# Twelve of sixteen maximum scans of w_in moved from the second attention stage into units 32 to 39 of the first

## The chip, the cores and the metric

One core of a Trainium2 chip runs the whole program. The metric is device time in microseconds (us), the median of three runs. TensorE (PE) does the matrix products and transposes, VectorE (DVE) and ScalarE (ACT) the elementwise work, GpSimd (POOL) a few additions and small casts, and the queue of SyncE (SP) issues every transfer. Each engine works through its own instructions in a fixed order and waits on semaphores of the others.

## The reference, cut to what matters

Attention with a learned position bias, then an MLP with a squared ReLU. The setup is four batches, eight heads, 576 positions, head width 64, and an MLP from 512 to 2048 and back.

```python
scores = scale * np.matmul(q, k.transpose(0, 1, 3, 2))
h = np.maximum(x @ w1 + b1, 0.0)          # x: log distance over log position
scores = scores + (h @ w2).transpose(2, 0, 1)[None]
attn = np.exp(scores - np.max(scores, axis=-1, keepdims=True))
attn = attn / (np.sum(attn, axis=-1, keepdims=True) + 1e-09)
x = np.matmul(attn, v)                    # rows of all heads side by side
r = np.maximum(x @ w_in, 0.0)
return (r * r) @ w_out
```

## The kernel before, in words

Attention is cut into 80 **units**: a batch b, a pair of heads hp and a chunk ic of 128 query rows (chunk 4 is the short tail of 64 rows). Units 0 to 39 take batches 0 and 1, chunk by chunk: the tail chunk in units 0 to 7, then chunks 0, 1, 2 and 3 in units 8 to 15, 16 to 23, 24 to 31 and 32 to 39. Units 40 to 79 take batches 2 and 3, five units for each pair of heads and batch. The MLP follows.

A unit has these steps. `score_products` (L421) writes two pairs of PSUM banks, `sp`, of which there is one set: the products of the next unit wait until VectorE has read those of this one. `softmax` reads them with one VectorE instruction for each head (L431, two in a full unit, one in a tail unit), and ScalarE takes the exponential (L436). Two units later TensorE transposes the result (L524, L516), ScalarE copies it (L827 in the first stage, L1041 in the second), and TensorE multiplies by v (L542); VectorE copies the sum to `xT` (L555). At the end of a head pair the row sums are inverted (L448, L449) and multiplied in (L491).

In units 0 to 30 the bias network runs beside this: VectorE masks (L371) and products (L387), TensorE sums (L381), GpSimd additions into the bias table (L395). Its tiles lie in the pool `prep`. It has nothing left to do from unit 31 on.

The MLP works on scaled halves of w_in and x. The scale of w_in comes from its largest absolute value: `scan_w` (L202, one VectorE reduction over 512 columns) for each of 16 tiles of 512 KB, that are fetched only for this (L662), then `top_w`. Before the change all 16 scans run in the second stage, as a job from unit 41 on, with five tiles in flight; `scan(k)` fetches the tile five further on into the place that it has just read. Only once all are done do the other jobs follow: `get` fetches the weights again, `in_job` splits them (L193 on ScalarE, L195, L196, L198, L199 on VectorE, L706 to L708 and L720 on GpSimd, L718 on ScalarE, L724 on VectorE), and `x_scaled` splits x (L765 on GpSimd, L771 on ScalarE, L778 on VectorE).

Two things set the order. In units 0 to 39 a scheduler places the instructions on each engine, by its own estimate of when each could start; only the score products are pinned. From unit 40 on the order is written by hand: `fill` takes jobs in the order of their list into each unit, as long as the allowance `room["DVE"]` (1.65 us more for each full unit, 2.5 for a tail unit) is not used up. `dest_at` says from which unit the first halves of w_in may be written over parts of the bias table that are no longer read.

Of the kernel before, what the change touches and what calls it, by code (L numbers as in the profile page):

```python
# [27 lines left out]
AB = 2  # L28
# [49 lines left out]
def attention_then_relu2_mlp(ctx: ExitStack, tc: tile.TileContext, q, k, v, cols, w_in, w_out, psi, xmat, dist, out):  # L78
# [729 lines left out]
    def ends(u):  # L808
        b, hp, ic = units[u]
        return ic == (chunks[-1] if u < NA else NIC - 1)  # L810

    rest = theta_steps(128, 512)[2:]
    for s in range(NA):
        loads(s)
        scores(s)
# [21 lines left out]

    prep_stack.close()
    half_stack.close()
# [79 lines left out]
    def scan(k):  # L919
        scan_w(k)  # L920
        if k + len(raws) < NF:
            fetch_in(ins[k + len(raws)], raws[k % len(raws)])
        if k == NF - 1:
            jobs.insert(len(norms), [now[0] + 1, [("DVE", 0.75, lambda: power_job(now[0] + 1, top_w(), scaled))]])
            for n in early[:4]:
                get(n)
            for _ in range(3):
                next_job()
            job(now[0], ("SP", 0, lambda: get(2), lambda: all((0, m) in xs_t for m in ORDER)))
# [15 lines left out]
    def x_scaled(n, ps_col):  # L945
        scale_of(n, ps_col)
        if n == 0:
            place_x = raw_tile("w2")
            free = [place_x[:, 512 * k:512 * k + 512] for k in range(2)]
            for k, ms in enumerate(((3, 1, 7), (4, 6), (2, 5))):  # L950
                stages = []
                for m in ms:
                    if RIGHT[m][1]:
                        sum_at[m] = free[k].rearrange("p (c t) -> p c t", c=2)
                        stages.append(("POOL", 1.3, lambda m=m: sums_x(0, (m,))))
                    stages.append(("ACT", 0.71, lambda m=m: high_x(0, (m,))))
                    stages.append(("DVE", 0.74, lambda m=m: low_x(0, (m,))))
                jobs.insert(len(norms), [now[0], stages])

    dest_at = [53] + [60] * 6 + [70]  # L960
    order = list(early[:7]) + [2, early[7], 3]
# [49 lines left out]
    with tc.manual_schedule():  # L1011
        job(NA + 1, *(("DVE", 0.68, lambda k=k: scan(k)) for k in range(NF)))
        x_job(NA + 4, 0)
# [6 lines left out]
        for s in range(NA, NU + TL + 2):  # L1020
            now[0] = s
            full = s < NU and units[s][2] < TAIL
            room["DVE"] = min(room.get("DVE", 0), 0.3) + (1.65 if full else 2.5)
            room["ACT"] = min(room.get("ACT", 0) + (0.55 if full else 1.9), 0.6 if full else 1.5)
            loads(s)
            if s == NA:
                for m, tag in enumerate(raws):
                    fetch_in(ins[m], tag)
            if s < NU:
# [292 lines left out]
```

## Time and profile before

| | |
|---|---|
| median of three runs | 724.46 us (724.44 to 724.8) |
| profiled execution | 724.39 us |
| its span, first to last instruction | 722.6 us |
| PE busy | 691.2 us, 96% |
| VectorE busy | 554.6 us, 77% |
| ScalarE busy | 474.8 us, 66% |
| GpSimd busy | 186.6 us, 26% |
| granted TensorE clock | full speed in every stretch to 700 us |

Unit 32 begins at about 161.8 us, unit 40 at 189.5 us, and the MLP at 343.4 us. The 1.8 us between the span and the profiled execution's time lie around the program. A table of stretches shows busy time of each engine in a stretch; where TensorE's busy time is short of the stretch, or its units are further apart than in other stretches with the same work, time is lost.

### The profile page before, as it was taken

The page shows a single profiled execution, that of the slowest core. Times are in us where ns is not written, and L with a number is a line of the kernel's source. Part 1 is how long each engine was busy: PE and PEld are TensorE (multiplying, and loading weights), DVE is VectorE, ACT ScalarE, POOL GpSimd, SP SyncE. Part 2 cuts the span into 40 slices and gives each one's busy share as a digit, 9 for nine tenths or more (in the row PEclk, how much of TensorE's full clock was granted, in tenths as well). Part 3 has the DMA queues.
Part 4 walks back from the last instruction along what each step waited for, and adds up shares of the span by engine and source line. Part 5 has one row for each costly group of instructions (what it writes and reads, how often), then busy time and mean ns, then how long its engine had stood idle before and what let it go on. Part 6 is the DMA issues. An engine that isn't in the chain of part 4 may idle for free.

```text
span 722.6 us, 17384 instructions
## 1 busy us (share of the span) xinstructions
PE 691.2 (96%) x6966; PEld 565.0 (78%) x6966; DVE 554.6 (77%) x1165; ACT 474.8 (66%) x954; POOL 186.6 (26%) x313
## 2 busy tenths in 40 slices
PE   7799999999999999899999999999999999999992
PEld 6577777787777877678878888888888888888881
DVE  8998888775588999889898969777468875566761
ACT  5678778777587888798666766666465564454220
POOL 6563433331110156444332304112011111000000
PEclk9999999999999999999999999999999999999997
DMA  6640000004449521410613333050067303533100
GB/s 187 200 123 3 19 2 2 3 2 118 169 162 286 163 85 36 136 60 14 236 59 161 147 160 117 8 212 1 1 201 294 134 14 134 187 117 117 59 2 29
DMA packets 31620, 75.13 MB, mean 104 GB/s; under 512 B 5556, under 2 KB 13876, under 8 KB 30516
## 3 DMA queue, kind: packets, MB, share of 16 engines
q1 hardware_dynamic: 31540, 74.03, 30.5%
q8 instruction: 55, 0.90, 0.5%
q14 instruction: 25, 0.20, 0.1%
HBM read 55.66 MB, written 18.35 MB: 102 GB/s over the span
## 4 chain that ended last, share of the span: by engine, by line
PE 79%; DVE 12%; ACT 4%; issue 2%; DMA 1%; ACTq 0%; DVEq 0%
PE y L1198 26%; PE ha L1103 12%; PE sp L421 9%; PE px L542 9%; PE hb L1103 9%; PE pp L524 8%; PE bb L381 4%; DVE t L431 2%; DVE mask L371 2%; ACT pt L1041 1%; PE pa L516 1%; ACT p L436 1%; DVE bt L387 1%; DMA raw<-in_w_in 1%; DVE wa L198 1%
## 5 line engine op out<-in xcount | busy, mean ns | idle before, releaser
L1103 PEld LDWEIGHTS <-area 128*128 128x128 f16 x1680 | 147.7, 98 | 25.1 <-issue 8.4
L1198 PE MATMUL y<-w,gh 128*128 128x512 f32 x576 | 149.1, 398 | 1.2 <-ACT gh L1142 1.2
L431 DVE CUSTOM_DVE_ANT_0 t<-sp,area 128x576 f32<-128x576 f32 x144 | 104.3, 752 | 26.0 <-PE sp L421 16.6
L1198 PEld LDWEIGHTS y<-w,gh 128*128 128x128 f32 x576 | 105.0, 188 | 23.4 <-ACT gh L1142 2.2
L436 ACT ACTIVATE p<-t,negm 128x576 f32<-128x576 f32 x144 | 111.9, 787 | 12.5 <-DVE negm L431 11.8
L421 PE MATMUL sp<-k,q 64*128 64x288 f32 (+1 forms) x640 | 98.5, 425 | 4.0 <-DVE negm L431 3.2
L542 PE MATMUL px<-pt,v 128*64 128x128 f32 (+1 forms) x1600 | 92.2, 266 | 1.6 <-DVE xT L491 0.8
L542 PEld LDWEIGHTS px<-pt,v 128*64 128x64 f32 x1600 | 79.2, 137 | 17.6 <-ACT pt L1041 7.1
L1103 PE MATMUL ha<-area 128*128 128x256 f16 (+1 forms) x816 | 84.8, 260 | 0.3 <-DVE c L1120 0.3
L524 PE MATMUL pp<-ident,p 128*128 128x128 f32 x576 | 78.9, 277 | 2.9 <-DVE xT L491 1.7
L1198 PE MATMUL y<-w,gl 128*128 128x512 f32 x288 | 79.0, 390 | 0.0
L395 POOL TENSOR_TENSOR area<-bt,bt 128x256 f32<-128x256 f32 x72 | 53.6, 767 | 78.5 <-DVE bt L387 78.5
L524 PEld LDWEIGHTS pp<-ident,p 128*128 128x128 f32 x576 | 62.2, 141 | 13.2 <-issue 7.5
L421 PEld LDWEIGHTS sp<-k,q 64*128 64x128 f32 (+1 forms) x640 | 53.3, 175 | 24.3 <-issue 5.7
L1103 PE MATMUL hb<-area 128*128 128x256 f16 (+1 forms) x612 | 65.0, 260 | 0.0
L1198 PEld LDWEIGHTS y<-w,gl 128*128 128x128 f32 x288 | 54.1, 188 | 12.2 <-DVE gl L1143 0.2
L371 DVE TENSOR_TENSOR mask<-sdist,theta 128x1024 f16<-128x1024 f16 x81 | 55.8, 726 | 5.6 <-PE bb L381 5.2
L381 PEld LDWEIGHTS <-mask 128*128 128x128 f16 x1296 | 42.3, 100 | 12.2 <-DVE mask L371 6.8
L381 PE MATMUL bb<-wmov,mask 128*128 128x64 f16 x1296 | 47.4, 196 | 4.4 <-DVE mask L371 4.1
L1041 ACT COPY pt<-pp 128x512 f32<-128x512 f32 x76 | 41.1, 602 | 15.2 <-PE pp L524 15.1
L827 ACT COPY pt<-pp 128x512 f32<-128x512 f32 x68 | 37.7, 588 | 14.4 <-PE pp L524 14.4
L1143 DVE TENSOR_TENSOR gl<-area,gh 128x512 fp32r<-128x512 f32 (+1 forms) x40 | 25.4, 668 | 26.3 <-ACT gh L1142 24.2
(164 smaller groups left out, 987.7 us busy)
## 6 DMA issues: line engine op xcount, KB each, us to landing
raw<-in_w_in SPq DMA_DIRECT2D x32, 512.0 KB, 4.5
r<-in_w_out SPq DMA_DIRECT2D x16, 512.0 KB, 5.5
xs<-area SPq DMA_DIRECT2D x4, 1792.0 KB, 11.9
py<-o SPq DMA_DIRECT2D x12, 512.0 KB, 2.7
o<-py SPq DMA_DIRECT2D x12, 512.0 KB, 4.4
v<-in_v SPq DMA_DIRECT2D x16, 320.0 KB, 4.2
q<-in_q SPq DMA_DIRECT2D x32, 128.0 KB, 3.0
out<-o SPq DMA_DIRECT2D x8, 512.0 KB, 2.9
```

The costliest lines, as they stand in the source:

```text
L371: DVE.tensor_tensor(out=out, in0=win, in1=th, op=ALU.is_ge)
L381: PE.matmul(bb[:, 64 * (7 - r):64 * (8 - r)], lhsT=m[:, r], rhs=wmov[:, n], start=(n == 0), stop=(n == 1))
L395: POOL.tensor_tensor(out=dst, in0=tw, in1=sw, op=ALU.add)
L421: mm = PE.matmul(out_t[to, x, :HALF], lhsT=qt[rows, cols], rhs=kt[rows, k0:k0 + HALF], start=True, stop=True)
L431: DVE.tensor_tensor_reduce(out=t.rearrange("p (x n) -> p x n", x=2), in0=sp[:, :, :HALF], in1=bias.rearrange("p (x n) -> p x n", x=2), sca ...
L436: ACT.activation(out=p[:, S * n:S * n + S], in_=t, func=AF.Exp, bias=negm[:, n:n + 1], scale=-1.0, accum_out=sums[:, 2 * ic + n:2 * ic + n ...
L524: PE.transpose(pp[:, 128 * c:128 * c + 128], p[:, k0:k0 + 128], ident)
L542: PE.matmul(px[64 * h:64 * h + 64, 128 * m:128 * m + w], lhsT=vt[:, c, h], rhs=src, start=(c == 0), stop=(c == 4))
L827: ACT.copy(dst, src)
L1041: ACT.copy(*c)
L1103: PE.matmul(h[:, s, :w], lhsT=a, rhs=x, start=(k == 0), stop=(k == 5))
L1198: PE.matmul(y_t[n][k], lhsT=(gl if m == 2 else gh)[:, slot, o:o + 128], rhs=wl if m == 1 else wh, start=((n, P) in firsts and f == 0 and m ...
```

## The change

Twelve of the sixteen scans are taken out of the job of the second stage. `scan_first` is called at the start of each of units 32 to 39: at unit 32 it closes `prep`, opens the pool `scan` of five tiles in its place and fetches five tiles; at units 34 to 39 it makes two scans each and fetches into the tiles that are scanned. The four last tiles are fetched at unit 40 and scanned as before. The allowance of VectorE per full unit becomes 1.5 us. The first destinations of w_in are free from unit 50, where it was 53, and the splits of x start at unit 51 at the earliest.

```diff
--- before.py
+++ after.py
@@ -809,8 +809,23 @@
         b, hp, ic = units[u]
         return ic == (chunks[-1] if u < NA else NIC - 1)
 
+    scan_stack, SCANS = ExitStack(), 12
+
+    def scan_first(s):
+        n = s - AB * HP * TAIL
+        if n == 0:
+            prep_stack.close()
+            stage_p["scan"] = scan_stack.enter_context(tc.tile_pool(name="scan", bufs=1, side="left"))
+        fetched_now = range(5) if n == 0 else range(2 * n + 1, min(2 * n + 3, SCANS)) if n >= 2 else ()
+        for k in range(2 * n - 4, min(2 * n - 2, SCANS)) if n >= 2 else ():
+            scan_w(k)
+        for k in fetched_now:
+            fetch(ins[k], stage_p["scan"].tile([128, 1024], F32, name="raw", tag=f"s{k % 5}", bufs=1))
+
     rest = theta_steps(128, 512)[2:]
     for s in range(NA):
+        if s >= AB * HP * TAIL:
+            scan_first(s)
         loads(s)
         scores(s)
         if s and rest:
@@ -835,7 +850,7 @@
             if waiting and waiting[0][:2] != (b, hp):
                 scale_x(*waiting.pop(0))
 
-    prep_stack.close()
+    scan_stack.close()
     half_stack.close()
     aux_stack.close()
     bank_stack = ExitStack()
@@ -919,7 +934,7 @@
     def scan(k):
         scan_w(k)
         if k + len(raws) < NF:
-            fetch_in(ins[k + len(raws)], raws[k % len(raws)])
+            fetch_in(ins[k + len(raws)], raws[(k - SCANS) % len(raws)])
         if k == NF - 1:
             jobs.insert(len(norms), [now[0] + 1, [("DVE", 0.75, lambda: power_job(now[0] + 1, top_w(), scaled))]])
             for n in early[:4]:
@@ -955,9 +970,9 @@
                         stages.append(("POOL", 1.3, lambda m=m: sums_x(0, (m,))))
                     stages.append(("ACT", 0.71, lambda m=m: high_x(0, (m,))))
                     stages.append(("DVE", 0.74, lambda m=m: low_x(0, (m,))))
-                jobs.insert(len(norms), [now[0], stages])
-
-    dest_at = [53] + [60] * 6 + [70]
+                jobs.insert(len(norms), [max(now[0], first[groups[AB * HP + AB]] + 1), stages])
+
+    dest_at = [50] + [60] * 6 + [70]
     order = list(early[:7]) + [2, early[7], 3]
     raw_of = dict(zip(early, ("stage", "stage", "zw", "w3", "stage", "stage", "zw", "stage")))
     after = {early[0]: early[4], early[1]: early[5], early[2]: early[6], early[3]: 3, early[4]: early[7]}
@@ -1009,7 +1024,7 @@
 
     sum_at = {}
     with tc.manual_schedule():
-        job(NA + 1, *(("DVE", 0.68, lambda k=k: scan(k)) for k in range(NF)))
+        job(NA + 1, *(("DVE", 0.68, lambda k=k: scan(k)) for k in range(SCANS, NF)))
         x_job(NA + 4, 0)
         x_job(NA + 7, 1)
         for b, hp, rows_t in waiting:
@@ -1020,12 +1035,12 @@
         for s in range(NA, NU + TL + 2):
             now[0] = s
             full = s < NU and units[s][2] < TAIL
-            room["DVE"] = min(room.get("DVE", 0), 0.3) + (1.65 if full else 2.5)
+            room["DVE"] = min(room.get("DVE", 0), 0.3) + (1.5 if full else 2.5)
             room["ACT"] = min(room.get("ACT", 0) + (0.55 if full else 1.9), 0.6 if full else 1.5)
             loads(s)
             if s == NA:
-                for m, tag in enumerate(raws):
-                    fetch_in(ins[m], tag)
+                for m, tag in enumerate(raws[:NF - SCANS]):
+                    fetch_in(ins[SCANS + m], tag)
             if s < NU:
                 negm, sps = score_products(s, False)
             fill(s, 3)
```

The three places below show the built order. `raw` is a tile of w_in, `small` holds the columns of maxima, `sp` the score products, `t` the scores with bias, `xT` the attention output.

VectorE, from the copy behind the softmax of unit 31 to just ahead of the softmax of unit 33, before:

```order
L555 COPY xT_82<-px 128x128
L431 ISA t,negm<-sp,area 128x576
L431 ISA negm 128x1
L431 ISA t,negm<-sp,area 128x576
L431 ISA negm 128x1
L555 COPY xT_83<-px 128x128
L448 TENSOR_SCALAR sums<-sums 128x9
L449 RECIPROCAL sums<-sums 128x9
```

and after:

```order
L555 COPY xT_82<-px 128x128
L202 TENSOR_REDUCE small<-raw 128x1 x2
L431 ISA t,negm<-sp,area 128x576
L431 ISA negm 128x1
L431 ISA t,negm<-sp,area 128x576
L431 ISA negm 128x1
L202 TENSOR_REDUCE small<-raw 128x1
L555 COPY xT_83<-px 128x128
L202 TENSOR_REDUCE small<-raw 128x1
L448 TENSOR_SCALAR sums<-sums 128x9
L449 RECIPROCAL sums<-sums 128x9
L202 TENSOR_REDUCE small<-raw 128x1
```

The scheduler has put the first two scans ahead of the softmax of unit 32, and three more ahead of that of unit 33, though the code calls the first at unit 34; two stand ahead of each of the softmaxes of units 34, 35 and 36, and one ahead of that of unit 37.

The queue of SP, behind the last load of the bias network, before (k and q are the first loads for batch 2):

```order
L129 DMA xc<-in_xmat 128x576 x3
L154 DMA k_3507<-in_k 64x576
L155 DMA k_3507<-in_k 64x640
L167 DMA q_3510<-in_q 64x64
L168 DMA q_3510<-in_q 64x4x128
```

and after:

```order
L129 DMA xc<-in_xmat 128x576 x3
L662 DMA raw<-in_w_in 128x1024 x6
L154 DMA k_3527<-in_k 64x576
L662 DMA raw<-in_w_in 128x1024
L155 DMA k_3527<-in_k 64x640
L167 DMA q_3530<-in_q 64x64
L168 DMA q_3530<-in_q 64x4x128
L167 DMA q_3530<-in_q 64x64
L168 DMA q_3530<-in_q 64x4x128
L662 DMA raw<-in_w_in 128x1024 x2
```

The first fetch waits for the last addition of the bias network on GpSimd (L395). Seven fetches now stand ahead of or among the first group of k and q; the next two are followed by the second group, then three more by the third.

VectorE in units 66 and 67, from the inversion behind the softmax of unit 65 to just ahead of the softmax of unit 67, before:

```order
L448 TENSOR_SCALAR sums<-sums 128x9
L449 RECIPROCAL sums<-sums 128x9
L724 SCALAR_TENSOR_TENSOR area<-wa,small,area 128x256
L724 SCALAR_TENSOR_TENSOR area<-raw,small,area 128x640
L555 COPY xT_3903<-px 128x256
L431 ISA t,negm<-sp,area 128x576
L431 ISA negm 128x1
L431 ISA t,negm<-sp,area 128x576
L431 ISA negm 128x1
L778 SCALAR_TENSOR_TENSOR area<-raw,small,area 128x512
L724 SCALAR_TENSOR_TENSOR area<-wa,small,area 128x256
L724 SCALAR_TENSOR_TENSOR area<-raw,small,area 128x640
```

and after:

```order
L448 TENSOR_SCALAR sums<-sums 128x9
L449 RECIPROCAL sums<-sums 128x9
L724 SCALAR_TENSOR_TENSOR area<-wa,small,area 128x256
L724 SCALAR_TENSOR_TENSOR area<-raw,small,area 128x640
L555 COPY xT_3943<-px 128x256
L431 ISA t,negm<-sp,area 128x576
L431 ISA negm 128x1
L431 ISA t,negm<-sp,area 128x576
L431 ISA negm 128x1
L195 TENSOR_SCALAR wa<-wa 128x512
L196 TENSOR_SCALAR wa<-wa 128x512
```

Unit 66 holds the same work; in unit 67 two short conversions of weights stand where a split of x and two of w_in stood, since those splits have moved to earlier units.

## Rows read from the trace of the kernel before

**Rows 1.** The page: busy time and share of the span of each engine.

```profile
PE 691.2 (96%) x6966; PEld 565.0 (78%) x6966; DVE 554.6 (77%) x1165; ACT 474.8 (66%) x954; POOL 186.6 (26%) x313
```

**Rows 2.** Stretches: length; PE, PEld, DVE, ACT, POOL busy; clock, DMA share, GB/s.

```profile
161.80:189.50 27.70, 27.41 (x291) 20.64 (x290) 16.23 (x52) 20.65 (x54) 5.33 (x28) 1.00 0.42 117
203.30:254.90 51.60, 50.68 (x597) 40.65 (x591) 45.68 (x121) 39.88 (x103) 7.10 (x29) 1.00 0.71 215
272.00:309.70 37.70, 33.25 (x384) 26.37 (x384) 33.67 (x73) 31.29 (x76) 20.87 (x32) 1.00 0.26 82
```

**Rows 3.** TensorE in order of time, score products of units 32, 33, 34, 37.

```profile
161.79 1.24 PE L421 MATMUL sp<-k,q 64*128 64x288 f32 x8
...
165.34 1.24 PE L421 MATMUL sp<-k,q 64*128 64x288 f32 x8
...
168.88 1.24 PE L421 MATMUL sp<-k,q 64*128 64x288 f32 x8
...
179.43 1.24 PE L421 MATMUL sp<-k,q 64*128 64x288 f32 x8
```

**Rows 4.** VectorE in order of time: the softmax of unit 32, start of unit 33's.

```profile
163.22 0.76 DVE L431 CUSTOM_DVE_ANT_0 t<-sp,area 128x576 f32<-128x576 f32 x1 [2.15 <-PE sp L421]
...
163.90 0.75 DVE L431 CUSTOM_DVE_ANT_0 t<-sp,area 128x576 f32<-128x576 f32 x1
...
166.62 0.76 DVE L431 CUSTOM_DVE_ANT_0 t<-sp,area 128x576 f32<-128x576 f32 x1 [0.53 <-PE sp L421]
```

**Rows 5.** GpSimd in order of time: the last additions of the bias network.

```profile
157.51 2.10 POOL L395 TENSOR_TENSOR area<-bt,bt 128x256 f32<-128x256 f32 x3 [2.76 <-DVE bt L387]
```

**Rows 6.** The page, transfers: issues of w_in, KB each, median us to landing.

```profile
raw<-in_w_in SPq DMA_DIRECT2D x32, 512.0 KB, 4.5
```

**Rows 7.** The tile raw, 182 to 236 us: the scans' idle wait; landing times of fetches.

```profile
  DMA raw<-in_w_in: 1.1, 2
...
DMA to landing us min/median/max: 3.2/5.4/8.0
```

**Rows 8.** Stretches as in rows 2: k, q groups alone; fetches alone; both together.

```profile
163.00:178.00 15.00, 15.00 (x166) 11.71 (x166) 8.89 (x31) 10.98 (x28) 1.98 (x10) 1.00 0.47 124
190.00:194.00 4.00, 4.00 (x54) 3.10 (x52) 1.11 (x3) 2.46 (x7) 0.18 (x1) 1.00 1.00 395
218.00:226.00 8.00, 7.71 (x94) 5.89 (x90) 7.14 (x17) 5.39 (x16) 0.79 (x4) 1.00 1.08 238
```

**Rows 9.** Line L202, the scans of the second stage: min/median/max in ns.

```profile
L202 DVE TENSOR_REDUCE small<-raw x16: 629/680/686, 202.8 to 231.5; 128x1 f32<-128x512 f32 x16
```

**Rows 10.** TensorE in order of time, score products of units 42, 47, 57, 62, 67, 72, 77.

```profile
203.34 1.24 PE L421 MATMUL sp<-k,q 64*128 64x288 f32 x8
...
221.23 1.24 PE L421 MATMUL sp<-k,q 64*128 64x288 f32 x8
...
254.86 1.24 PE L421 MATMUL sp<-k,q 64*128 64x288 f32 x8
...
272.04 1.24 PE L421 MATMUL sp<-k,q 64*128 64x288 f32 x8 [0.20 <-DVE negm L431]
...
291.13 1.24 PE L421 MATMUL sp<-k,q 64*128 64x288 f32 x8 [0.94 <-DVE negm L431]
...
309.74 1.24 PE L421 MATMUL sp<-k,q 64*128 64x288 f32 x8 [0.20 <-DVE negm L431]
...
326.56 1.24 PE L421 MATMUL sp<-k,q 64*128 64x288 f32 x8
```

**Rows 11.** Line L199, the last step of a weight's conversion: min/median/max in ns.

```profile
L199 DVE SCALAR_TENSOR_TENSOR wa<-raw,wa x16: 691/692/1649, 252.0 to 575.4; 128x512 uint32<-128x512 uint32 x16
```

**Rows 12.** VectorE in order of time: splits of x and w_in ahead of unit 67's softmax.

```profile
290.90 1.52 DVE L778 SCALAR_TENSOR_TENSOR area<-raw,small,area 128x512 f16<-128x512 f32 x1
...
292.75 0.87 DVE L724 SCALAR_TENSOR_TENSOR area<-raw,small,area 128x640 f16<-128x640 f32 x1
```

**Rows 13.** GpSimd in order of time, in the same stretch.

```profile
290.61 1.27 POOL L765 TENSOR_TENSOR xT<-xT 128x512 f32<-128x512 f32 x1
```

## The prediction

> **What bounds the kernel now.** I read the page first: TensorE is busy for 96% of the span [rows 1], so time can only come from, or go into, stretches where it idles or its units stand further apart than they must. The table of stretches says where. While units 32 to 39 run, TensorE is busy for 27.41 of 27.7 us, VectorE for only 16.23 [rows 2]: there is room on VectorE, and none on TensorE. From 203.3 to 254.9 us, where the scans run now, TensorE is busy for 50.68 of 51.6 us; from 272.0 to 309.7 us for 33.25 of 37.7 [rows 2]. So the scans' own stretch loses little, and the loss sits later, among the splits of weights and x.
>
> The starts of the score products measure that loss with no model of busy time. Five units (four full, one tail) are one period, so starts five units apart hold the same work. Units 47 to 57 take 254.86 - 221.23 = 33.63 us, 16.8 for each five, and units 72 to 77 take 16.8 again [rows 10]: that is the clean period. Units 42 to 47 take 17.9, 57 to 62 take 17.2, 62 to 67 take 19.1 and 67 to 72 take 18.6 [rows 10]. Above 16.8 that is 1.1 + 0.4 + 2.3 + 1.8 = 5.6 us, all that a lighter VectorE can win back here. The rows at units 62, 67 and 72 name VectorE's softmax as what TensorE waited for.
>
> **What is removed.** Twelve scans of 0.68 us [rows 9] are 8.2 us of VectorE. They leave units 42 to 50, and from unit 47 on these already run at the clean period, though two scans waited 1.1 us in all for their fetches [rows 7]; what hides them there is TensorE's own work. Taking them out wins nothing at their place. What it does is let the later jobs start some four units sooner and, with 1.5 us instead of 1.65 a unit, lie thinner. 0.15 us less in 32 full units is 4.8 us of allowance, less than the 8.2 us of work gone, so nothing spills past the last unit.
>
> How much of the 5.6 us returns I read from the built order. In unit 67 two short conversions stand where three splits stood, as shown. In unit 63, too, a split of x and a pair of conversions (L195, L196) give way to nothing, and in unit 70 four conversion steps to two splits. But unit 66 holds the same work as before, unit 62 as well, and in unit 60 the pair L198 and L199 replaces the shorter L195 and L196. Three of the six heavy places get lighter, so I take half, **2.8 us gained**. The ends are 0 and 5.6: no loss, since VectorE has less to do in all, and no more than what is there.
>
> **What is added, and what waits.** The first fetch waits for the last bias addition, which ends at 157.51 + 2.10 = 159.6 us [rows 5]. The fastest fetch landed 3.2 us after its issue, the median one 5.4 [rows 7]. The first in an idle queue should be near the fast end; I take 3.4, which gives 163.1 us. Behind it, fetches alone move 395 GB/s [rows 8], so 512 KB [rows 6] follow each 1.33 us.
>
> VectorE meets the first scans too early. In the built order two stand ahead of the softmax of unit 32, which before began at 163.22 us and ended at 163.90 + 0.75 = 164.65 [rows 4]. Tile 1 lands at 163.1 + 1.33 = 164.4, its scan ends at 165.1, the two softmax instructions (1.43 us) at 166.5. Queued behind the waiting scan are that softmax and, on TensorE, the next score products, which need the PSUM that it reads: those of unit 33 go from 165.34 [rows 3] to 166.6, **1.2 us late**. Tiles 2 to 4 stand ahead of the softmax of unit 33. Tile 4 lands at 168.4, its scan ends at 169.1, the softmax at 170.5, and the products of unit 34 start at 170.6 in place of 168.88 [rows 3]: 1.7 late.
>
> The queue then sets the pace. Two more tiles are ahead of each of the next softmaxes, up to tile 10 ahead of that of unit 36, and by then two groups of k and q loads stand between them. These three groups moved in 163 to 178 us before, at a mean DMA share of 0.47 [rows 8]: 0.47 x 15 / 3 = 2.35 us of full transfer for a group. Tile 10 lands at 163.1 + 10 x 1.33 + 2 x 2.35 = 181.1, the softmax of unit 36 ends at 183.2, and the products of unit 37 begin at 183.3 instead of 179.43 [rows 3]: 3.9 late. TensorE has 0.3 us to spare in this stretch [rows 2], so the delay stays, and everything behind shifts with it.
>
> That sum lets k, q and fetches take turns without cost. The trace of before does not show them so in this stretch, but it has one with both, where the engines were full and moved 238 GB/s instead of 395 [rows 8]. If all from tile 5 (169.8 us) to tile 10 went at that rate, it would be five tiles of 0.524 MB and two groups of 124 GB/s x 15 us / 3 = 0.62 MB, 3.86 MB in 16.2 us. Tile 10 would land at 186.0 us, and the products of unit 37 come 8.8 us late. So the cost lies between 1.2 (only the first pair ever holds) and 8.8 us. I take **5.0 us lost**, nearer to 3.9 than to 8.8: tiles are fetched one by one as scans free them, so the mixture is not there all the time.
>
> Four other edits cost nothing on the path. k and q for unit 40 now stand behind seven tiles, 9.3 us at 1.33 each, and still land well ahead of 189.5 us, where that unit began. The four scans left have their places in units 42 to 45, which had scans before. The destination limit and the later of two starts for the splits only allow what the thinner jobs would use.
>
> **The sum.** 724.39 us of the profiled execution + 5.0 - 2.8 = 726.6. The median of the runs shown is 0.07 us above that execution, which changes nothing: **726.6 us**, 0.3% slower.
>
> **Rivals.** *The relief does not come.* The slow VectorE instructions may not be slow for want of allowance. L199 takes 0.69 us in the median and 1.65 once [rows 11]; ahead of unit 67 a split took 1.52 us while GpSimd added pieces of x [rows 12, 13], and a wider one behind it 0.87 [rows 12]. The additions move along with the splits, to units with as much softmax. Then only about 0.8 of the 2.3 + 1.8 us around units 62 to 72 is won, and 724.39 + 5.0 - 0.8 = 728.6, or 732 with the full mixture of loads. Against it: unit 63 and unit 67 have spare time now in which a slow split is harmless. The Trainium skill, page "SBUF — State Buffer", section "Who interferes with whom", has a rule for it: a VectorE instruction with two SBUF inputs contends with a GpSimd instruction that reads SBUF, and a reduction never does. By that rule the change takes away only work that never collided, and keeps all that did, which would give this rival's 728.6. The rows above agree as far as the splits go; the scans' narrow spread of 629 to 686 ns agrees too [rows 9].
>
> *Both effects cancel.* If the transfers keep to 395 GB/s and the softmaxes of units 35 and 36 find their tiles landed, the loss is about 3 us and the gain about 3: 724.4 us.
>
> *Faster: the scans hold only the first pair.* If k and q slip into gaps, every tile from the third on is there when VectorE arrives, and the loss is 1.2 to 2 us. If with it the thinner allowance clears most of the four slow periods, 4.5 us, the time is 724.39 + 1.5 - 4.5 = 721.4. It decides at tile 10: if that lands before about 178 us, the products of unit 37 are less than 1.5 us late. For it speaks that VectorE had 11 us idle in this stretch [rows 2]; against it, that twelve tiles alone need 16 us at the full rate after a start at 159.6.
>
> **How the numbers follow.** About 0.2% (1.45 us) is what a measurement of this kernel can tell from no change: faster is below 723.0, slower above 725.9. My forecast, a loss of 3.9 to 6.5 and a gain of 1.5 to 4, gets 0.45; it runs from 724.3 to 729.4, and 0.38 of it lies above 725.9. No relief gets 0.15, all slower. Cancelling gets 0.12, the same. The faster case gets 0.28. So slower 0.38 + 0.15 = 0.53, same 0.07 + 0.12 = 0.19, faster 0.28. The range for 8 in 10 leaves out the lower part of the faster case (0.12) and the upper part of no relief (0.06): 721.8 to 729.8 us. Both signs are in it; the forecast's own range is 724.3 to 729.4.
>
> **What would show it.** In the profile of the changed kernel VectorE should idle ahead of L202 for "DMA raw" between 161 and 186 us, some 5 us in all, and TensorE's score products of units 33 to 38 should wait for VectorE. Unit 37 should start near 184.5 us, 5 later than before. Periods of five units above 16.8 us between units 57 and 72 should add up to about 2.8 us. I am wrong if the first stage shows no idle VectorE ahead of the scans, or if those periods all come down to 16.8, or stay where they are.

## The result, and the profile after

The changed kernel takes 732.72 us (median of four, 732.09 to 734.15), the kernel before in the same comparison 724.45 us (724.44 to 724.8): ratio 1.0117, 95% interval 1.0101 to 1.0133. It is slower, as forecast, but by 8.3 us and not by 2.2, and outside the range of 721.8 to 729.8 us. The profiled execution took 733.0 us.

First the table of stretches, the lines that answer to [rows 2] (length; PE, PEld, DVE, ACT, POOL busy; clock, DMA share, GB/s): units 32 to 39, 42 to 56, 57 to 61 and 62 to 71.

```profile
162.06:198.30 36.24, 30.99 (x291) 23.59 (x290) 23.21 (x64) 20.56 (x54) 5.37 (x28) 0.91 0.87 258
212.10:264.82 52.72, 51.33 (x598) 41.10 (x594) 45.13 (x127) 42.88 (x108) 11.43 (x29) 1.00 0.31 95
264.82:283.97 19.15, 16.32 (x203) 12.87 (x204) 17.08 (x37) 15.58 (x41) 14.59 (x25) 1.00 0.37 95
283.97:317.36 33.39, 32.79 (x385) 26.32 (x385) 27.39 (x69) 29.98 (x74) 11.15 (x25) 1.00 0.36 99
```

Units 32 to 39 took 27.75 us before and take 36.24 now: **8.5 us, the whole loss, lies there.** Units 42 to 79 take 129.81 us before and 129.82 after, from score products to score products: the later stage gave nothing.

The first stage, from VectorE in order of time (the answer to [rows 4]; the bracket is the idle time before an instruction and what ended it). L202 is a scan, L431 a softmax.

```profile
164.76 0.69 DVE L202 TENSOR_REDUCE small<-raw 128x1 f32<-128x512 f32 x1 [3.42 <-DMA raw<-in_w_in]
165.90 0.69 DVE L202 TENSOR_REDUCE small<-raw 128x1 f32<-128x512 f32 x1 [0.45 <-DMA raw<-in_w_in]
166.50 0.75 DVE L431 CUSTOM_DVE_ANT_0 t<-sp,area 128x576 f32<-128x576 f32 x1
...
174.77 0.69 DVE L202 TENSOR_REDUCE small<-raw 128x1 f32<-128x512 f32 x1 [1.42 <-DMA raw<-in_w_in]
175.37 0.75 DVE L431 CUSTOM_DVE_ANT_0 t<-sp,area 128x576 f32<-128x576 f32 x1
...
180.67 0.69 DVE L202 TENSOR_REDUCE small<-raw 128x1 f32<-128x512 f32 x1 [1.68 <-DMA raw<-in_w_in]
181.27 0.75 DVE L431 CUSTOM_DVE_ANT_0 t<-sp,area 128x576 f32<-128x576 f32 x1
...
184.41 0.69 DVE L202 TENSOR_REDUCE small<-raw 128x1 f32<-128x512 f32 x1 [1.50 <-DMA raw<-in_w_in]
...
186.01 0.69 DVE L202 TENSOR_REDUCE small<-raw 128x1 f32<-128x512 f32 x1 [0.59 <-DMA raw<-in_w_in]
186.62 0.75 DVE L431 CUSTOM_DVE_ANT_0 t<-sp,area 128x576 f32<-128x576 f32 x1
```

Each of these four softmaxes (units 32, 34, 35 and 36) stands right behind a scan that waited for its tile. The view of the tile `raw` from 160 to 200 us sums that up (idle time and count, then landing times), against 1.1 us in [rows 7]:

```profile
  DMA raw<-in_w_in: 10.7, 9
...
DMA to landing us min/median/max: 3.3/5.9/8.2
```

And TensorE in order of time (the answer to [rows 3]): score products of units 32, 33, 34, 36 and 37, with the products with v (L542) of two of them.

```profile
162.06 1.24 PE L421 MATMUL sp<-k,q 64*128 64x288 f32 x8
163.24 1.31 PE L542 MATMUL px<-pt,v 128*64 128x128 f32 x20
...
168.08 1.24 PE L421 MATMUL sp<-k,q 64*128 64x288 f32 x8 [2.40 <-DVE negm L431]
169.25 2.37 PE L542 MATMUL px<-pt,v 128*64 128x128 f32 x20
...
173.25 1.24 PE L421 MATMUL sp<-k,q 64*128 64x288 f32 x8
...
182.85 2.20 PE L421 MATMUL sp<-k,q 64*128 64x288 f32 x8 [2.28 <-DVE negm L431]
...
188.19 1.24 PE L421 MATMUL sp<-k,q 64*128 64x288 f32 x8 [0.19 <-DVE negm L431]
```

This execution runs 0.28 us behind that of before when unit 32 starts. Unit 33 is then 2.5 us late, unit 37 is at 188.19 in place of 179.43, **8.5 us late**, and stays so up to unit 47. The stretches of 3 us show what the transfers did meanwhile (columns as above; the last two are DMA share and GB/s):

```profile
163.00:166.00 3.00, 2.68 (x33) 2.04 (x29) 0.79 (x2) 0.09 (x1) 0.00 (x0) 1.00 1.02 416
166.00:169.00 3.00, 0.92 (x8) 0.78 (x8) 3.00 (x8) 1.71 (x5) 0.00 (x0) 1.00 1.02 419
169.00:172.00 3.00, 3.00 (x26) 2.42 (x23) 2.74 (x9) 1.77 (x5) 1.00 (x5) 0.55 1.05 298
172.00:175.00 3.00, 3.00 (x27) 2.35 (x27) 1.33 (x5) 2.02 (x7) 0.99 (x5) 0.88 1.16 218
175.00:178.00 3.00, 2.91 (x31) 2.23 (x27) 2.03 (x7) 1.84 (x5) 0.00 (x0) 1.00 1.02 327
178.00:181.00 3.00, 2.57 (x31) 2.04 (x29) 1.29 (x4) 0.91 (x3) 0.00 (x0) 1.00 0.95 212
181.00:184.00 3.00, 1.15 (x6) 1.01 (x8) 1.91 (x6) 1.94 (x5) 0.00 (x0) 0.83 0.98 287
184.00:187.00 3.00, 3.00 (x28) 2.07 (x25) 1.97 (x5) 0.81 (x3) 0.00 (x0) 0.60 1.06 293
```

The DMA engines are full throughout. Up to 169 us they carry 416 to 419 GB/s, nearly all of it tiles; from then on, with k and q among them (issued from 166.2 us, the first landed at 172.4), 212 to 327. Tile 10 landed at 185.99 us.

### The profile page after: what moved, and what is told of

Read it like the earlier page. It is cut to its first block, busy times and chain, and to the rows that moved or that the text cites. A ratio compares the mean times of both kernels' runs of the same rounds, so it can differ in the third digit from the quotient of the medians.

```text
span 731.2 us, 17390 instructions
## 1 busy us (share of the span) xinstructions
PE 693.4 (95%) x6966; PEld 566.2 (77%) x6966; DVE 554.2 (76%) x1165; ACT 474.7 (65%) x954; POOL 184.7 (25%) x313
## 4 chain that ended last, share of the span: by engine, by line
PE 74%; DVE 11%; DMA 4%; issue 4%; ACT 3%; POOL 1%; SPq 1%; ACTq 0%; DVEq 0%; POOLq 0%
PE y L1213 26%; PE ha L1118 12%; PE hb L1118 9%; PE px L542 8%; PE sp L421 8%; PE pp L524 6%; PE bb L381 4%; DMA raw<-in_w_in 3%; DVE t L431 3%; DVE mask L371 2%; PE pa L516 1%; DVE bt L387 1%; ACT p L436 1%; DVE wa L198 1%; DMA q<-in_q 1%
## 5 line engine op out<-in xcount | busy, mean ns | idle before, releaser
L431 DVE CUSTOM_DVE_ANT_0 t<-sp,area 128x576 f32<-128x576 f32 x144 | 104.2, 752 | 23.6 <-PE sp L421 11.6
L542 PE MATMUL px<-pt,v 128*64 128x128 f32 (+1 forms) x1600 | 93.9, 269 | 1.6 <-DVE xT L491 0.8
L542 PEld LDWEIGHTS px<-pt,v 128*64 128x64 f32 x1600 | 80.8, 139 | 18.0 <-ACT pt L1056 5.9
L395 POOL TENSOR_TENSOR area<-bt,bt 128x256 f32<-128x256 f32 x72 | 53.7, 770 | 78.4 <-DVE bt L387 78.4
L381 PE MATMUL bb<-wmov,mask 128*128 128x64 f16 x1296 | 45.8, 193 | 6.1 <-DVE mask L371 6.0
L381 PEld LDWEIGHTS <-mask 128*128 128x128 f16 x1296 | 40.5, 98 | 14.0 <-DVE mask L371 8.5
```

Of the source, the lines that this page charges most:

```text
L381: PE.matmul(bb[:, 64 * (7 - r):64 * (8 - r)], lhsT=m[:, r], rhs=wmov[:, n], start=(n == 0), stop=(n == 1))
L395: POOL.tensor_tensor(out=dst, in0=tw, in1=sw, op=ALU.add)
L431: DVE.tensor_tensor_reduce(out=t.rearrange("p (x n) -> p x n", x=2), in0=sp[:, :, :HALF], in1=bias.rearrange("p (x n) -> p x n", x=2), sca ...
L542: PE.matmul(px[64 * h:64 * h + 64, 128 * m:128 * m + w], lhsT=vt[:, c, h], rhs=src, start=(c == 0), stop=(c == 4))
```

## The experiments

Times in this section: the median, the ratio to the kernel before with its interval, and three distances between score products, from the profiled execution of each. That execution can lie off the median where a kernel scatters: it took 733.65 us in e2, 739.13 in e3 (the slowest of its four), 731.09 in e4 (the fastest) and 727.0 in e5. Before: 27.75 us for units 32 to 39, 13.80 for 40 and 41, 129.81 for 42 to 78 (to the start of unit 79). "Slow splits" is what VectorE's instructions from unit 47 to the start of unit 78 took above the shortest duration of the same line and shape, summed where it is over 0.15 us: 6.7 us before, 7.6 after. It holds more than the splits: of the 7.6 us, L724 and L778 make 2.9, the conversions L195, L196 and L198 3.7, the row sums (L448) 1.0.

| run | us | ratio, 95% interval | 32 to 39 | 40, 41 | 42 to 78 | slow splits |
|---|---|---|---|---|---|---|
| after | 732.72 | 1.0117 (1.0101 to 1.0133) | 36.24 | 13.80 | 129.82 | 7.6 |
| e1_resident | 723.67 | 0.9992 (0.9983 to 1.0001) | 27.75 | 13.80 | 129.76 | 7.6 |
| e2_pinned | 732.07 | 1.0112 (1.0097 to 1.0127) | 37.14 | 13.80 | 129.77 | |
| e3_kq_late | 735.83 | 1.0156 (1.0139 to 1.0173) | 42.50 | 13.81 | 129.81 | |
| e4_room165 | 733.90 | 1.0129 (1.0105 to 1.0153) | 34.96 | 13.80 | 129.82 | 3.4 |
| e5_behind12 | 726.59 | 1.0033 (1.0021 to 1.0046) | 27.75 | 16.67 | 129.83 | 7.6 |
| e6_behind5 | 719.89 | 0.9938 (0.9924 to 0.9953) | 27.75 | 13.03 | 126.62 | 4.7 |
| e7_fill_resident | 721.29 | 0.9962 (0.9948 to 0.9976) | 27.75 | 13.81 | 127.47 | 4.3 |
| e8_fill_before | 721.10 | 0.9956 (0.9941 to 0.9971) | 27.75 | 13.82 | 127.05 | 1.5 |
| e9_order_alone | 724.18 | 0.9996 (0.9987 to 1.0006) | 27.75 | 13.80 | 129.61 | 4.8 |
| e10_fill_behind5 | 719.68 | 0.9935 (0.9920 to 0.9950) | 27.75 | 13.03 | 126.09 | 2.5 |
| e11_behind5_165 | 723.58 | 0.9988 (0.9979 to 0.9998) | 27.76 | 13.02 | 130.08 | 5.5 |
| e12_behind9 | 722.43 | 0.9973 (0.9963 to 0.9982) | 27.93 | 13.02 | 128.54 | 6.2 |

**The transfers away, the scans kept (e1_resident).**

```diff
-            scan_w(k)
+            tc.keep_in_program_order(scan_w(k))
-            fetch(ins[k], stage_p["scan"].tile([128, 1024], F32, name="raw", ...))
+            wraw_t[ins[k]] = words(area[:, 0:1024])
```

> The twelve early scans read a slice of the bias table, which is in SBUF already, in place of a fetched tile: no w_in tile is fetched in units 32 to 39, and the scans are pinned to the place at which the program writes them. (The scale of w_in then leaves twelve of its tiles out; everything behind takes the same time.) VectorE does the same twelve reductions in units 33 to 40. Theory (the loss is waiting for transfers): the products of unit 37 start within 1 us of before's 179.43 us, plus whatever the first bias lines differ, and the whole time comes back to about 724.5 us (723.5 to 726), since the later stage gave nothing net. Rival (the loss is VectorE's extra 8.2 us of reductions ahead of softmaxes, whatever they wait for): unit 37 stays 4 us or more late and the time stays above 728 us.

723.67 us: the theory's number. VectorE does the twelve reductions among units 33 to 40 (20.59 us busy in the stretch, 16.23 in [rows 2]) and no unit there moves:

```profile
161.75:189.50 27.75, 27.46 (x292) 20.64 (x291) 20.59 (x60) 20.71 (x54) 5.33 (x28) 1.00 0.41 119
```

So the 8.5 us are not VectorE's work but its waiting. The edit also pins the scans, so they don't stand where the changed kernel has them: in this execution eight fall into the stretch, two of them right ahead of the softmax of unit 33 and two ahead of that of unit 38, and neither pair makes a unit late. The run also shows the later stage by itself: twelve scans less, and 129.76 us in place of 129.81.

**The scans where the program writes them (e2_pinned).**

```diff
-            scan_w(k)
+            tc.keep_in_program_order(scan_w(k))
```

> The changed kernel with one thing more: the twelve scans stay where the program writes them (one in unit 33, two in 35, three in 36, two in 38, four in 40 in the built order) instead of being hoisted ahead of the softmaxes of units 32 to 37. Fetches and computation are those of the changed kernel. Theory (hoisted scans make the softmaxes wait for tiles not yet landed): most of the 8.5 us goes, unit 37 starts at most 3 us later than before, and the whole takes 724.5 to 727.5 us. Rival (the mixture of fetches with the k and q loads holds the units themselves, wherever the scans stand): unit 37 or unit 42 stays 5 us or more late and the time stays above 729 us.

732.07 us, by its number the rival's. But the edit did not do what the expectation says: it did not hold the scans at their places, and the scheduler put the scan of the fifth tile first, ahead of the softmax of unit 33. VectorE stood still for it:

```profile
171.97 0.69 DVE L202 TENSOR_REDUCE small<-raw 128x1 f32<-128x512 f32 x1 [5.75 <-DMA q<-in_q]
172.57 0.75 DVE L431 CUSTOM_DVE_ANT_0 t<-sp,area 128x576 f32<-128x576 f32 x1
```

The row names the last of several waits, a load of q; the fifth tile had landed at 171.79 us, just ahead of the scan. This wait and one of 3.04 us ahead of another scan make 8.8 us, and unit 37 is 9.4 late. The run decides nothing between the two; e5 repeats it properly.

**k and q later (e3_kq_late).**

```diff
-            if s == max(first[g] - KL, NA - AB * HP + 2 + m):
+            if s == max(first[g] - KL, NA if m in (1, 2) else NA - AB * HP + 2 + m):
```

> The changed kernel with the k and q loads of two of the three groups that stand among the fetches in units 34 to 39 issued at unit 40 instead. Theory (the mixture of k and q loads with fetches is what made my 5.0 us into 8.5): the tenth tile behind the first lands 4 to 5 us earlier than the 185.99 us of the changed kernel, unit 37 starts some 4 us late in place of 8.5, and the time falls from 732.7 to 728 to 729 us, if the two groups still land in time for units 45 to 55. Rival (the late first landing and the one-by-one refetch set the pace, not the mixture): less than 1.5 us comes back, 731 to 733 us.

735.83 us, against both. The loads were written later, but the scheduler issued them at 175.9 and 183.0 us all the same, and mixed single loads of k and q in between single fetches. One tile needed 11 us from issue (178.20) to landing (189.16); VectorE's idle time for tiles is 12.9 us. (The profiled execution is the slowest of the four, so the 42.50 us of the table are more than the median's.) The mixture was not taken away, so its share is not settled by this run.

**The allowance back (e4_room165).**

```diff
-            room["DVE"] = min(room.get("DVE", 0), 0.3) + (1.5 if full else 2.5)
+            room["DVE"] = min(room.get("DVE", 0), 0.3) + (1.65 if full else 2.5)
```

> The changed kernel with the allowance of VectorE's other work for each full unit put back from 1.5 to 1.65 us; the scans and the rest stay as changed. Theory (the slow units of the later stage are slow because single splits meet GpSimd's additions, and these meet wherever the jobs lie): the time is that of the changed kernel within 1 us, 731.7 to 733.7 us, and the periods of five units between 42 and 72 still lose some 5.6 us above 16.8 each, in other places. Rival (the thinner allowance itself moved the jobs into a worse or better place): 2 us or more of difference, either way.

733.9 us, from 731.09 to 735.28: the same within what this kernel scatters. Units 42 to 78 take 129.82 us with other units slow than after, and only 3.4 us of slow splits. Its first stage holds the same instructions as after and lost 7.2 us in the profiled execution, not 8.5: what waits for transfers differs from execution to execution. It fits that the kernels whose scans wait (after, e2, e3, e4) scatter by 2 to 4 us, and the kernel before by 0.4 to 1.2.

**Every scan behind a softmax (e5_behind12).**

```diff
+        last_softmax[0] = DVE.tensor_tensor_reduce(...)
+    def scan_behind(s):
+        with tc.issue_after(last_softmax[0].ins):
+            for k in {2: (0, 1), 3: (2, 3), 4: (4,), 5: (5, 6), 6: (7, 8), 7: (9, 10, 11)}.get(s - AB * HP * TAIL, ()):
+                scan_w(k)
+                if k + 5 < SCANS:
+                    fetch(ins[k + 5], stage_p["scan"].tile(...))
```

> The changed kernel, all twelve fetches and scans in it, but each scan is queued on VectorE behind the softmax of a later unit: tiles 0 and 1 behind that of unit 34, 2 and 3 behind 35, 4 behind 36, 5 and 6 behind 37, 7 and 8 behind 38, 9 to 11 behind 39; each refetch stands behind the scan that frees its buffer. In the built order no scan stands ahead of a softmax whose unit it delays by a tile not yet asked for. Theory (the loss is scans that wait for tiles in front of softmaxes; the transfers themselves harm nobody): VectorE's idle time ahead of the scans falls from 10.7 us to under 3 us, unit 40 starts at most 3 us later than before's 189.54 us, and the whole takes 724 to 727 us. Rival (the fetches also hold up k and q, and so the units, whatever VectorE waits for): unit 40 or 42 stays 5 us or more late, 729 us or above.

726.59 us, the theory's number. The stretch of units 32 to 39 takes 27.75 us as before, with the DMA engines nearly full and TensorE's clock at its upper level:

```profile
161.95:189.70 27.75, 27.45 (x292) 20.65 (x291) 21.15 (x61) 20.74 (x54) 5.38 (x28) 1.00 0.90 292
```

Ten of the twelve tiles land in it, mixed with the same k and q, and nobody is late. What is left is in unit 40, where tiles 10 and 11 came last, again ahead of work for which TensorE waits (L493 is the multiplication by the row sums):

```profile
191.78 0.69 DVE L202 TENSOR_REDUCE small<-raw 128x1 f32<-128x512 f32 x1 [1.83 <-DMA raw<-in_w_in]
193.03 0.69 DVE L202 TENSOR_REDUCE small<-raw 128x1 f32<-128x512 f32 x1 [0.57 <-DMA raw<-in_w_in]
193.63 0.68 DVE L493 TENSOR_TENSOR xT<-xT,ra 128x512 f32<-128x512 f32 x1
```

TensorE waited for it and then ran at a lower clock:

```profile
194.37 0.64 PE L487 MATMUL ra<-rows,pick 128*64 128x128 bf16 x8 [2.02 <-DVE xT L493]
...
194.99 1.97 PE L526 MATMUL pp<-ident,p 128*128 128x128 f32 x8
```

The same eight transposes took 1.09 us before. TensorE had been busy for 0.63 of the 2 us from 193 us on, and the granted clock from 195 to 198 us was 0.53. The 2.9 us lost in unit 40 are this wait (2.1 us later than before at L487) and the slow pieces behind it (1.5), less a wait of 0.8 us that unit 40 had before and has no more.

**Five scans, no refetch (e6_behind5).** The same edit with SCANS = 5 and the places `{3: (0, 1), 4: (2, 3), 5: (4,)}`.

> As the run with twelve scans behind the softmaxes, but with only the five tiles that need no refetch: 0 and 1 behind the softmax of unit 35, 2 and 3 behind 36, 4 behind 37; the other eleven are scanned in the later stage, as before. Theory (only waiting in front of softmaxes costs): nothing is lost up to unit 40 (189.54 us within 0.3) and the whole takes 723 to 725.5 us, no faster than the kernel before by more than 0.2%, since the later stage gave nothing for twelve scans less. Rival (lighter VectorE does help the later stage once nothing is lost ahead of it): 720 to 722.5 us.

719.89 us: the rival's number, **0.6% faster than the kernel before**, and the fastest of the runs that leave nothing out. Nothing is lost up to unit 40, and VectorE waits for none of the five tiles. 0.8 us come back in unit 40, where a wait of TensorE for VectorE (L542 for L491, 0.8 us) is gone, and 3.2 us in units 42 to 78. The rival had a reason for it, less work on VectorE; the next five runs are on that.

**GpSimd without additions (e7_fill_resident, e8_fill_before, e10_fill_behind5).** One edit, made in e1_resident, the kernel before, and e6_behind5:

```diff
+    def fill_in(n):
+        POOL.memset(blocks_in(n)[1], 0.0)
+    def fill_x(n, m):
+        for cs, op, a, b in halves(n, m):
+            POOL.memset(sum_of(n, m)[:, :, cs], 0.0)
...
-                        stages.append(("POOL", 1.3, lambda m=m: sums_x(0, (m,))))
+                        stages.append(("POOL", 1.3, lambda m=m: fill_x(0, m)))
...
-            ("POOL", 2.0, lambda: sums_in(n)),
+            ("POOL", 2.0, lambda: fill_in(n)),
```

> The kernel with resident scans (no fetches in the first stage, VectorE's later stage as in the changed kernel), in which GpSimd fills the places of the sums of x and of w_in with zeros in units 40 to 79 instead of adding or subtracting two pieces; all other instructions stay in their order. (The sums of these weights and of the first x are left out, so their values are not the reference's; every later step works on them as before.) Theory (what slows units 42 to 79 is VectorE's splits running long beside GpSimd's additions, 7.6 us above their shortest in the changed kernel): splits come down to their shortest durations, and the starts of units 49 to 79 come together by 3 to 6 us, 718 to 721 us. Rival (the units are slow from VectorE's plain load or ScalarE's, not from slow splits): 723 to 724.5 us, as with the additions.

> The kernel before with the same zero fills in place of GpSimd's sums of w_in and of the first x in units 40 to 79 (these sums are left out). Theory (slow splits beside additions make the slow units): VectorE's 6.7 us above the shortest durations goes, the four slow periods around units 57 to 72 lose most of their 5.6 us, 719 to 721.5 us; and if the kernel with resident scans gets to the same time or lower by under 1 us, then taking the scans out of the later stage is worth that and no more. Rival (load): 723.5 to 725 us here, while the resident kernel with fills is 2 us or more faster than this one.

> The run with five scans behind softmaxes, with GpSimd's sums of w_in and of the first x in units 40 to 79 replaced by zero fills (these sums are left out), everything else in its order. Theory (its gain over the kernel before is that its splits meet fewer additions, 4.7 us above their shortest in place of 6.7, and these 4.7 us still cost): 717 to 718.5 us, 1.5 to 3 us below its 719.9. Rival (its gain has nothing to do with the additions): 719.5 us or above.

Without the additions the resident kernel is 2.4 us faster (723.67 to 721.29), the kernel before 3.3 (724.38 to 721.10), and the fast one 0.2 (719.89 to 719.68), where I had expected 1.5 to 3: there the rival holds, and the additions lie where they cost nothing. The resident kernel with fills is 0.3 us above the theory's span, the kernel before with fills inside it.

Where the additions cost shows beside the resident kernel with fills, which has the changed kernel's order on VectorE and ScalarE from unit 42 on. Two units are 1 us or more shorter there (and unit 55 is 0.6 longer): unit 52 (4.29 us in the changed kernel, 3.31 with fills), by two slow conversions ahead of its softmax that the last section names, and unit 58 (4.76 and 3.30). Ahead of the softmax of unit 58 ScalarE waits for GpSimd's sum and VectorE for ScalarE. ScalarE and VectorE first, then GpSimd, then TensorE's products of units 58, 59 and 60:

```profile
268.53 0.72 ACT L771 ACTIVATE area<-raw,small 128x512 f16<-128x512 f32 x1 [1.36 <-POOL raw L765]
...
269.28 1.12 DVE L778 SCALAR_TENSOR_TENSOR area<-raw,small,area 128x512 f16<-128x512 f32 x1 [1.26 <-ACT area L771]
...
272.00 1.60 DVE L724 SCALAR_TENSOR_TENSOR area<-wa,small,area 128x256 f16<-128x256 f32 x1
273.52 1.89 DVE L724 SCALAR_TENSOR_TENSOR area<-raw,small,area 128x640 f16<-128x640 f32 x1
```

```profile
272.05 1.27 POOL L765 TENSOR_TENSOR raw<-xT 128x512 f32<-128x512 f32 x1
273.40 1.34 POOL L765 TENSOR_TENSOR xT<-xT 128x512 f32<-128x512 f32 x1
```

```profile
268.16 1.24 PE L421 MATMUL sp<-k,q 64*128 64x288 f32 x8 [0.28 <-DVE negm L431]
...
272.93 1.19 PE L421 MATMUL sp<-k,q 64*64 64x288 f32 x8
...
276.63 1.24 PE L421 MATMUL sp<-k,q 64*128 64x288 f32 x8
```

The split at 269.28 us is only 0.4 us slow; ScalarE's wait of 1.36 us, behind which VectorE idles for 1.26, is most of the loss. The two splits that follow, L724, are 2.2 us slow beside the additions, and that costs nothing: unit 59 takes 3.7 us here and with fills. There the same pair (L727) takes:

```profile
261.54 0.48 DVE L727 SCALAR_TENSOR_TENSOR area<-wa,small,area 128x256 f16<-128x256 f32 x1
261.94 0.88 DVE L727 SCALAR_TENSOR_TENSOR area<-raw,small,area 128x640 f16<-128x640 f32 x1
```

The fills wait for no input and are shorter than the additions (0.52 us in place of 1.28 for a piece of x), so these runs take away two things at once: the slow splits, and ScalarE's wait for the sums. In the kernel before, the slow pieces themselves cost: unit 62 takes 4.20 us, with fills 3.31, and ahead of its softmax L198 and L199 took 1.08 and 1.65 us, with no idle time of VectorE between. And with the additions gone in both, the kernel without twelve scans in the later stage (721.29) is no faster than the one with them (721.10).

**The order alone (e9_order_alone, e11_behind5_165).** e9 is the kernel before with the change's three small edits (first destination at unit 50, the later start for x, an allowance of 1.6 us); e11 is e6 with the allowance at 1.65.

> The kernel before, all sixteen scans in the later stage as before and no fetch in units 32 to 39; only the three small edits of the change: the first destination at unit 50 in place of 53, the later of two starts for the splits of x, and the allowance of a full unit 1.6 us in place of 1.65 (at 1.5 the jobs don't fit into the units). Theory (what the later stage loses depends on which unit each split falls into and what GpSimd does beside it, not on the sum of VectorE's work): the time may move by up to 4 us either way although VectorE does the same work; a gain of 1.5 us or more would show it. Rival (five scans less, 3.4 us of VectorE, are what made the run with five scans behind softmaxes 4.5 us faster): no gain here, 723.7 to 725 us or slower.

> The run with five scans behind softmaxes, with the allowance of a full unit at before's 1.65 us in place of 1.5. VectorE's work is the same. Theory (the meeting of splits and additions decides): the time differs from 719.9 us by 1 us or more, most likely upwards, 721 to 724.5 us, and VectorE's time above the shortest durations changes in the same direction. Rival (less VectorE work in the later stage is the gain): 719 to 720.7 us.

e9: single units start up to 1.9 us late and 0.7 early, counted from unit 32, and 724.18 us come out, no change, the rival's number. e11 speaks against that rival: 723.58 us, 3.7 more than e6 with exactly the same work, so the work taken from VectorE is not by itself what made e6 fast. One place where they differ, units 58 and 59. In e11 a split of x and a conversion, both slow, stand between the softmax of unit 57 and that of unit 58, for which the products of the tail unit 59 wait (L433 is the softmax here):

```profile
258.29 1.00 DVE L780 SCALAR_TENSOR_TENSOR area<-raw,small,area 128x512 f16<-128x512 f32 x1
259.21 1.49 DVE L195 TENSOR_SCALAR wa<-wa 128x512 f32<-128x512 f32 x1
```

```profile
258.46 1.24 PE L421 MATMUL sp<-k,q 64*128 64x288 f32 x8 [0.23 <-DVE negm L433]
262.89 1.19 PE L421 MATMUL sp<-k,q 64*64 64x288 f32 x8 [0.41 <-DVE negm L433]
```

In e6 the slow piece is a conversion behind the softmax of unit 58, and unit 59's products, which no longer wait for VectorE then, started 3.31 us after those of unit 58, not 4.43:

```profile
257.44 1.24 PE L421 MATMUL sp<-k,q 64*128 64x288 f32 x8
260.75 1.19 PE L421 MATMUL sp<-k,q 64*64 64x288 f32 x8
```

```profile
260.21 1.73 DVE L198 SCALAR_TENSOR_TENSOR wa<-raw,wa 128x512 int32<-128x512 int32 x1
```

**Nine scans (e12_behind9).** The edit of e5 without its last place, SCANS = 9.

> As the run with twelve scans behind softmaxes, with nine (tiles 0 to 8): the last three, whose tiles landed at 188.5 to 193.0 us and held VectorE 2.4 us in unit 40, go to the later stage. Theory (a transfer costs only where a scan waits for it ahead of other work): nothing is lost up to unit 41 (199.6 us within 0.5); the whole then depends on the later stage, 719 to 724.5 us. Rival (the fetches delay the later stage's own loads): unit 41 or 42 starts 2 us or more late, 726 us or above.

722.43 us, within the theory's span: unit 41 starts at 199.38 us (199.59 before), VectorE waits 0.6 us for a tile, and the later stage, in its own order, gives 1.3 us.

## Why the prediction was wrong, point by point

**The place and the mechanism of the loss: right.** VectorE idled ahead of scans, the softmaxes stood behind them, and unit 37 was late. Without the fetches the loss is gone (e1), and without a scan in front of a softmax it is gone although all tiles move (e5).

**Its size: the term that was mis-sized.** The step that failed is the choice of 5.0 us, "nearer to 3.9 than to 8.8", on the ground that tiles are fetched one by one and "the mixture is not there all the time". It was there from 169 us on. From the first landing to that of tile 10 the engines were full (a DMA share of 1.03) and moved 306 GB/s on average, 277 after 169 us. That took 21.4 us, where the sum had 18.0 with turns and 22.9 with 238 GB/s. The first step was short too: the first tile landed 4.7 us after its issue (159.91 to 164.59), not 3.4, which adds 1.5 us. Tile 10 landed at 185.99 us, where the upper end had 186.0 and the lower 181.1; that it met the upper end so closely is in part luck, since the mixture was faster than 238 GB/s and the first tile later than forecast. Unit 33 was 2.5 us late in place of 1.2, unit 37 8.5. The row with fetches and other loads together, 238 GB/s [rows 8], was at hand, and I discounted it.

**The edits costed at nothing: right.** k and q came in time: units 40 and 41 take 13.80 us in both kernels.

**The gain of 2.8 us: wrong, it is 0.** The step that failed is reading relief from the built order by counting heavy units that get lighter. They did get lighter: units 62 to 71 take 33.39 us in place of 37.70 [rows 2, 10], 4.3 us won. But other units got heavier, and I did not cost those. Units 57 to 61 take 19.15 us in place of 17.18, 47 to 56 34.84 in place of 33.63, 72 to 78 24.56 in place of 23.41: 1.97 + 1.21 + 1.15 = 4.3 lost. My own sign, that the periods from unit 57 to 71 stand about 2.8 us above 16.8 us for each five, came close (2.1 us, 4.5 before) and misled all the same: it left out the units on either side.

**The rival that came true** is "the relief does not come" with the full mixture of loads, 732 us, to which I gave 0.15. Its mechanism is only part of it, and its number is in part luck: it let units 62 to 72 give only 0.8 us, and they gave 4.3. Splits do meet GpSimd's additions in the new order too (7.6 us of slow splits after, 6.7 before), and the additions cost 2.4 to 3.3 us in two of the three orders tried, by slow splits and by ScalarE's wait for the sums together. By the rule that I cited from the Trainium skill, page "SBUF — State Buffer", section "Who interferes with whom", the scans never collided, so that taking them out wins nothing; the 129.76 us of e1 agree with the outcome. But with the additions gone, taking the scans out, in the change's order, still won nothing (e7 and e8). What the later stage loses depends on which unit each job falls into more than on the sum of VectorE's work: with twelve scans gone it takes as long as with all sixteen, and with five gone it takes 126.62 us in one order and 130.08 in another.

**What stays open.** Why the order of e6 loses 3.2 us less than before is shown at one place (units 58 and 59), not as a rule that could be worked out ahead; neither load nor the sum of slow splits ranks the orders (e4 has 3.4 us of slow splits and no gain). That units 42 to 78 came to 129.8 us in three different orders (before, after, e4) I take for chance; e9 and e11 differ. How much of the 8.5 us the mixture makes by itself was not isolated, since e3 didn't remove it; nor was the order in SP's queue, where the fetches of tiles 9 and 10 (issued at 178.65 and 180.71 us) stand behind the second group of k and q.

## What to carry to other kernels

An instruction that waits for a transfer holds everything behind it on its engine, so a load that only fills idle time must be used behind the urgent work, not ahead of it, and a scheduler that goes by its own estimate of the landing may put it ahead unless it is told otherwise: the same twelve tiles cost 8.5 us in front of the softmaxes; behind them they cost nothing up to unit 40, and 2.9 us there, where the last two came late. Where two kinds of transfer have shared the engines anywhere in the trace, weigh the rate of that row as much as the sum with turns: here 21.4 us were measured, 22.9 by that rate and 18.0 with turns. And when work is taken off an engine with an order written by hand, count what the moved jobs make heavier as well as what they make lighter: here five scans less won 3.2 us in the later stage in one order and lost 0.3 in another, and twelve less won nothing.

## What the runs showed of the hardware

- TensorE's clock fell after it had stood still. In the changed kernel it was busy for 0.92 of 3 us from 166 to 169 us, and the granted clock of the next 3 us was 0.55, near the lower of its two levels (1.2 and 2.4 GHz); the 20 products with v that took 1.31 us in unit 32 took 2.37. It happened again at 184 us (0.60; score products 2.20 us in place of 1.24). These slow pieces added 1.6 us of TensorE's time twice, which I had not put into the sum. They did not set unit 37's start, since VectorE waited for tile 10 until 185.99 us anyway.
- 416 GB/s for tiles alone in 163 to 166 us and 419 in the next 3 us, in which the first load of k was issued (166.24), above the 395 of [rows 8].
- VectorE's instructions with one tensor input, L195 and L196, are slowed beside GpSimd as well: 0.89 and 1.38 us at 246.66 and 247.58 us in the changed kernel, where 0.37 and 0.43 are their shortest, while two additions (L765) ran for 2.69 us.
